# Gate and val of a gated MLP made for two token blocks together, on 512-column matmuls, with w_out2 fetched from DRAM

## The chip, the cores and the metric

One core of one Trainium2 chip runs the whole program. The metric is the device time of one execution in microseconds (us). PE is TensorE (the matrix engine), DVE is VectorE, ACT is ScalarE, POOL is GpSimd; SP is SyncE, whose queue issues all DMA transfers here.

## The reference, cut to what matters

A linear attention makes the 4608 x 512 matrix x; two MLPs follow. Their weights come as 64-bit floats.

```python
# first MLP: w_in 512 x 2048, w_out 2048 x 512
h = x @ w_in
x = (h * np.clip(h + 3.0, 0.0, 6.0) / 6.0) @ w_out
# second MLP: w_gate, w_val 512 x 1536, w_out2 1536 x 512
xn = x / np.sqrt(np.mean(x * x, axis=-1, keepdims=True) + 1e-06) * rms_g
g = xn @ w_gate
val = xn @ w_val
return (g * (1.0 / (1.0 + np.exp(-g))) * val) @ w_out
```

## The kernel before, in words

**Precision.** Each matmul operand is split in a high part (rounded to the matmul's format by ACT, `hi_of`, L197) and a low part (what is left, subtracted by DVE or POOL, `lo_of`, L203). A product of two operands is three matmuls: high with high, high with low, low with high (`PAIRS`).

**Blocks and stages.** The tokens stand in nine blocks of 512 columns. The first 936 us hold the attention, the conversion of the weights from 64 bits, the first MLP (`m1`, `prod1`, `m2`) and the norm of each block (`y_...`, L672 to L706), which is stored to DRAM as `xn_d`. From about 936 us on runs the stage that the change is about: gate, val, silu(gate) x val, and the product with `w_out2` (`m4`), block after block.

**Seven products in place of eight.** Gate and val are made by a Winograd scheme. A pair `i` (of six) takes two chunks of 128 output columns of both w_gate and w_val. Over the halves of the 512 inputs, the two chunks and the two halves of the tokens it is a 2 x 2 by 2 x 2 product, done with seven products `prod(j, i, k)`, k in the order 1, 6, 5, 2, 7, 3, 4. Block `j` of 512 tokens has token halves of 256 columns, and one product makes gate and val side by side in one PSUM bank: 2 (gate, val) x 2 (128-row input chunks) x 3 = 12 matmuls of 256 columns. The weight operand of product k (a sum of parts of w_gate and w_val) is fetched from DRAM as `pg` and split into `phu` and `plu`; seven of the 42 stay in SBUF for all blocks, the others are fetched and split again for each block. The operand from the tokens is one of `xb` and `ut` (sums of parts of xn), split into `xhu` and `xlu`.

**What hangs on a product.** The sums go into three PSUM banks, `pux` (products 1 and 2), `puy` (6, 7, 4) and `puz` (5, 3). After product 1 ACT copies pux (`c_copy`, L838); DVE adds puy to that copy as c12 (after 6), puz as c22 (after 5), puy to c22 (after 7), puz to c12 (after 3), and puy to c21 (after 4), all `c_add` (L845). Product 7 waits for the first c12, product 3 for the first c22, **product 4 for the second c22**, since each of them writes on into the bank that was read. Then come silu on ACT (L868), the multiplication (L873) and the split of the result u into `uh` and `ul`.

**w_out2.** Its 12 chunks of 128 rows lie in SBUF as `hout` and `lout` for the whole stage. `m4(j, i)` multiplies chunk i: 4 token groups x 3 = 12 matmuls of 512 columns, into four PSUM banks `o`.

**What sets the order.** PE's steps are written out in the list `seq`; a chunk step stands after products 2 and 4 of each pair (`merge`). Everything else is a task with needs, a duration and a due step; `Plan.emit` places the tasks on the engines by these numbers as the program is built, and each engine and the SP queue then run their instructions in that order. Rooms are counted there too: 77 SBUF tiles of 2 KB a partition (`unit`), 8 of 4 KB (`wide`), four rotating PSUM banks. `step(h - n)` lets a task begin n steps of `seq` ahead of step h. LEAD, XLEAD and WLEAD are such leads.

Of the kernel before, what the change touches and what calls it, by code (L numbers as in the profile page):

```python
# [24 lines left out]
XLEAD = 2  # L25
WLEAD = 10
# [102 lines left out]
def kernel(  # L129
# [21 lines left out]
    B, H, S, D = q.shape  # L151
# [7 lines left out]
    T = S // P  # L159
    TAIL = S - T * P  # L160
    NP1 = NF // 4
    NP2 = NF2 // 2
    HALF = NB // 2
    EPS = 1e-9
# [288 lines left out]
    def runs(j):  # L453

        done = 0
        while done < P:
            b, s = divmod(j * NB + done * NQ, S)
            step = min(P - done, (S - s) // NQ)
            yield done, done + step, b, s
            done += step  # L460
# [244 lines left out]
    def y_store(j, c):  # L705
# [28 lines left out]
        "u": [(i, k) for k in (4, 3, 7, 2, 5, 6, 1) for i in range(NP2)][:7],  # L734
# [23 lines left out]
    def couples(i):  # L758

        gone = [[k for k in c if (i, k) not in KEEP["u"]] for c in ((1, 6), (5, 2), (7, 3), (4,))]  # L760
        return [(k,) for k in ORDER if (i, k) in KEEP["u"]] + [tuple(c) for c in gone if c]
# [12 lines left out]
    def p_src(l, j, i, k):  # L774
        return wsrc(l, i, k) if l == "h" else pw[j, i, k]

    def p_hi(l, j, i, k):
# [5 lines left out]
        hi_of(wp[l, j, i, k][0], p_src(l, j, i, k))  # L783

    def p_lo(l, j, i, k, eng):
# [3 lines left out]
        lo_of(w[1], p_src(l, j, i, k), w[0], eng)  # L789
# [40 lines left out]
    def prod(j, i, k):  # L830
        product("u", j, i, k)

    def bank(l, j, i, n):
        return pb[l, j, i, n].rearrange("p z t -> p (z t)")

    def c_copy(l, j, i):
        cs[l, j, i, "c21"] = utile(f"c21{l}{j}_{i}")
        nc.scalar.copy(cs[l, j, i, "c21"], bank(l, j, i, "x"))  # L838

    def c_add(l, j, i, n, src, b):  # L840

# [11 lines left out]
    def load_xn(j, k, t):  # L853
# [10 lines left out]
    def u_silu(j, i, m, t):  # L864
# [465 lines left out]
```

## Time and profile before

| | |
|---|---|
| median of three runs | 1779.71 us (1774.97 to 1780.66) |
| profiled execution, its own time | 1777.19 us |
| its span, first to last instruction | 1775.4 us |
| mean granted TensorE clock | 0.994 |
| PE, weight loads, DVE, ACT, POOL busy | 97%, 87%, 77%, 53%, 15% of the span |

The profile is one execution of the program, with every instruction's start and duration. Of an engine's row the name is read as output<-inputs, with buffer numbers left out; "idle before" is the time in which the engine had nothing to do just before the row, with what released it. Durations of matmuls overlap, so what one costs is the distance from its start to the next one's. A granted clock of 1.00 is TensorE's level of 2.4 GHz, 0.50 that of 1.2 GHz; between them a stretch holds both.

### The profile page before, as it was taken

Reading aid. Unit: us, or ns where it says so; the run is one execution under the profiler, and the core shown is the slowest. Engines: PE = TensorE matmul, PEld = TensorE weight load, DVE = VectorE, ACT = ScalarE, POOL = GpSimd, SP = SyncE. Lnnn points to the kernel's source line nnn. Section 1 sums busy time; section 2 is a strip of 40 time slices with the busy share of each in tenths; the row PEclk is TensorE's granted clock in tenths of the full one; section 3 lists DMA queues with packets and bytes.
Section 4 is the critical chain, followed back from the end, with each engine's and each line's share of the span. In section 5 each row is a group of like instructions: output and inputs, shape, how many; then the busy total and the mean of one; then the engine's idle time right before and its main releaser. Section 6 shows DMA issues by size and latency. Waiting matters only on the chain.

```text
span 1775.4 us, 30493 instructions
## 1 busy us (share of the span) xinstructions
PE 1724.4 (97%) x11166; PEld 1543.7 (87%) x11166; DVE 1375.3 (77%) x2670; ACT 944.0 (53%) x2190; POOL 263.5 (15%) x254
## 2 busy tenths in 40 slices
PE   4899999999999999999999999999999999999999
PEld 3678878888888898888889899999999999999998
DVE  8897888888888888788686776767686768676764
ACT  7864566475565656555566444545444545454442
POOL 3254321011313223131111000000000000000000
PEclk9899999999999999999999999999999999999999
DMA  9656486996989888786872442424151524334230
GB/s 253 187 172 215 142 273 235 335 301 218 283 253 285 261 266 260 226 282 222 313 270 92 171 155 101 144 78 162 62 187 48 176 75 134 122 110 146 96 131 25
DMA packets 166278, 331.26 MB, mean 187 GB/s; under 512 B 23536, under 2 KB 78832, under 8 KB 166128
## 3 DMA queue, kind: packets, MB, share of 16 engines
q1 hardware_dynamic: 166128, 329.31, 56.5%
q8 instruction: 88, 1.44, 0.3%
q14 instruction: 62, 0.51, 0.1%
HBM read 267.91 MB, written 61.34 MB: 185 GB/s over the span
## 4 chain that ended last, share of the span: by engine, by line
PE 82%; DMA 7%; DVE 6%; ACT 2%; SPq 1%; issue 1%; ACTq 0%; DVEq 0%
PE y L655 17%; PE o L891 16%; PE puy L821 13%; PE puz L821 9%; PE pux L821 9%; PE h L596 6%; PE phy L821 4%; PE phz L821 3%; PE phx L821 3%; DMA q<-in_q_dram 2%; PE kvp L404 1%; DMA v<-in_v_dram 1%; DMA k<-in_k_dram 1%; DMA raw_gv<-in_moe_w_val_dram 1%; PE xps L552 1%
## 5 line engine op out<-in xcount | busy, mean ns | idle before, releaser
L203 DVE TENSOR_TENSOR plu<-pg,phu 128x512 fp32r<-128x512 f32 x317 | 217.0, 692 | 59.8 <-ACT phu L197 56.2
L821 PE MATMUL puy<-xhu,phu 128*128 128x256 f32 x648 | 183.5, 283 | 2.6 <-DVE c22u L845 2.6
L197 ACT ACTIVATE phu<-pg 128x512 fp32r<-128x512 f32 x322 | 184.4, 623 | 1.5 <-DMA pg<-pd 1.4
L821 PE MATMUL puy<-xhu,plu 128*128 128x256 f32 x648 | 183.8, 284 | 0.0
L821 PE MATMUL puy<-xlu,phu 128*128 128x256 f32 x648 | 183.8, 284 | 0.0
L891 PE MATMUL o<-hout,uh 128*128 128x512 f32 x432 | 170.2, 394 | 0.0
L891 PE MATMUL o<-lout,uh 128*128 128x512 f32 x432 | 169.6, 393 | 0.0
L891 PE MATMUL o<-hout,ul 128*128 128x512 f32 x432 | 168.4, 390 | 0.1
L655 PE MATMUL y<-gl,hout 128*128 128x512 f32 x360 | 142.3, 395 | 5.4 <-DVE gl L203 5.4
L655 PE MATMUL y<-gh,hout 128*128 128x512 f32 x360 | 144.4, 401 | 0.8 <-ACT ysb L668 0.8
L655 PE MATMUL y<-gh,wo 128*128 128x512 f32 x432 | 142.8, 391 | 0.0
L655 PE MATMUL y<-gh,lout 128*128 128x512 f32 x360 | 141.2, 392 | 0.0
L821 PEld LDWEIGHTS puy<-xhu,phu 128*128 128x128 f32 x648 | 124.4, 192 | 5.0 <-DVE c22u L845 2.8
L821 PEld LDWEIGHTS puy<-xlu,phu 128*128 128x128 f32 x648 | 124.6, 192 | 2.1
L845 DVE TENSOR_TENSOR c22u<-c22u,puy 128x512 f32<-128x512 f32 x54 | 37.1, 687 | 113.3 <-PE puy L821 113.3
L821 PEld LDWEIGHTS puy<-xhu,plu 128*128 128x128 f32 x648 | 124.6, 192 | 0.0
L868 ACT ACTIVATE u<-c22u 128x256 f32<-128x256 f32 x54 | 22.6, 418 | 188.2 <-DVE c22u L845 188.2
L821 PE MATMUL pux<-xhu,plu 128*128 128x256 f32 x432 | 122.3, 283 | 0.0
L821 PE MATMUL puz<-xlu,phu 128*128 128x256 f32 x432 | 122.3, 283 | 0.0
L821 PE MATMUL puz<-xhu,phu 128*128 128x256 f32 x432 | 122.3, 283 | 0.0
L821 PE MATMUL puz<-xhu,plu 128*128 128x256 f32 x432 | 122.2, 283 | 0.0
L821 PE MATMUL pux<-xlu,phu 128*128 128x256 f32 x432 | 122.2, 283 | 0.0
(254 smaller groups left out, 5037.1 us busy)
## 6 DMA issues: line engine op xcount, KB each, us to landing
pg<-pd SPq DMA_DIRECT2D x153, 512.0 KB, 6.1
wh<-rdh SPq DMA_DIRECT2D x126, 512.0 KB, 4.9
wo<-rdout SPq DMA_DIRECT2D x54, 512.0 KB, 4.3
raw_out<-in_moe_w_out_dram SPq DMA_DIRECT2D x28, 512.0 KB, 5.2
rdh<-hw SPq DMA_DIRECT2D x21, 512.0 KB, 4.5
v<-in_v_dram SPq DMA_DIRECT2D x72, 128.0 KB, 5.1
xn_d<-ysb SPq DMA_DIRECT2D x36, 256.0 KB, 3.6
xb<-xn_d SPq DMA_DIRECT2D x36, 256.0 KB, 3.6
```

The source lines that it names most:

```text
L197: nc.scalar.activation(hi, src, AF.Copy)
L203: on(engine).tensor_tensor(lo, src, hi.bitcast(F32), ALU.subtract)
L404: nc.tensor.matmul(ps[e * D:(e + 1) * D, u, s:s + D + 1], kk, vv, start=(u == 0 and t == 0), stop=(t == T), skip_group_check=True,)
L552: nc.tensor.matmul(ps[:, :, p0:p1], kvbd[b % 2][a][:, u, :], t[z][:, :, p0:p1], start=(n == 0), stop=(n == 2),)
L596: nc.tensor.matmul(hps[j, i], w[a][:, o:o + P], xs[j][b][u], start=(u == 0 and m == 0), stop=(u == C - 1 and m == 2),)
L655: nc.tensor.matmul(acc[j][c], w[a][:, c * P:(c + 1) * P], g[b], start=(i == 0 and n == 0), stop=(i == NF - 1 and n == 2),)
L821: nc.tensor.matmul(ps[:, z, :], w[a][:, o:o + P], x[b][:, c * HALF:(c + 1) * HALF], start=(first and z == 0 and c == 0 and m == 0), stop=( ...
L845: nc.vector.tensor_tensor(cs[l, j, i, n], t, bank(l, j, i, b), ALU.add)
L868: nc.scalar.activation(ut[j, ch][:, t * HALF:(t + 1) * HALF], c_part("u", j, i, m, t, 0), AF.Silu)
L891: nc.tensor.matmul(acc["o", j][c], u[a][:, c * P:(c + 1) * P], w[b], start=(i == 0 and n == 0), stop=(i == NF2 - 1 and n == 2),)
```

## The change

Blocks 1 to 8 are taken in four couples (`SUPER`: block 0 alone, then 1 and 2, 3 and 4, 5 and 6, 7 and 8). For a couple, the scheme's two token halves are the two whole blocks, so that a half has 512 columns, and gate (z = 0) and val (z = 1) are products of their own: `prod(S, i, z, k)` is 2 x 3 = 6 matmuls, with 512 columns in a couple and 256 in block 0. Seven products of gate come ahead of seven of val; I call such seven a group. Block 0 has 12 groups, each couple 12.

Weight operands are fetched in DRAM's new layout by half (gate or val) and by two products at once, and split once for each couple; none stays in SBUF. Token operands of a couple are 1024 columns wide and lie in wide tiles. The silu of gate is made while val is computed. The 12 chunks of w_out2 are split into wide tiles during block 0, put to DRAM after their use there, and fetched from there (512 KB each) for each of the eight other blocks. A pair of chunk steps follows from a queue, one pair to a group, and none where none is ready: in block 0 after every second group, in the first couple at first too; the last seven pairs come after all products. Planned durations of PE's steps are raised: `m1`, `m2` and `m4` from 2.6 to 2.73, `prod1` from 1.31 to 1.44.

```diff
-XLEAD = 2
-WLEAD = 10
+XLEAD = 9
+ULEAD = 7
+WLEAD = 9
...
+    SUPER = [(0,), *((j, j + 1) for j in range(1, NJ, 2))]
+    COUPLES = ((1, 6), (5, 2), (7, 3), (4,))
...
-    def p_put(i, ks, z):
+
+
+    def p_put(i, ks, n):
         if (i, ks) not in w_d:
-            w_d[i, ks] = dram.tile([P, len(ks), NB], F32, name=f"pd{i}_{ks[0]}")
-        nc.sync.dma_start(w_d[i, ks][:, z], wsrc("u", i, ks[z]))
-
-    def p_get(j, i, ks):
-        t = wtile(f"pg{j}_{i}_{ks[0]}", F32, (P, len(ks), NB))
-        nc.sync.dma_start(t, w_d[i, ks])
-        for z, k in enumerate(ks):
-            pw[j, i, k] = t[:, z]
-
-    def p_src(l, j, i, k):
-        return wsrc(l, i, k) if l == "h" else pw[j, i, k]
+            w_d[i, ks] = dram.tile([P, 2, len(ks), HALF], F32, name=f"pd{i}_{ks[0]}")
+        nc.sync.dma_start(w_d[i, ks][:, :, n], wsrc("u", i, ks[n]).rearrange("p (z f) -> p z f", z=2))
+
+    def p_get(S, i, z, ks):
+        pw[S, i, z, ks] = utile(f"pg{S}_{i}{z}_{ks[0]}", F32, (P, len(ks), HALF))
+        nc.sync.dma_start(pw[S, i, z, ks], w_d[i, ks][:, z])
+
...
-    def prod(j, i, k):
-        product("u", j, i, k)
+    def prod(S, i, z, k):
+
+        first = k in (1, 6, 5)
+        n = NB if len(SUPER[S]) == 2 else HALF
+        if first:
+            pb["u", S, (i, z), BANK[k]] = ptile(f"pu{BANK[k]}{S}_{i}{z}", (P, n))
+        ps, w, x = pb["u", S, (i, z), BANK[k]], wp["u", S, i, z, k], xo["u", S, k]
+        for c in range(2):
+            for m, (a, b) in enumerate(PAIRS):
+                nc.tensor.matmul(
+                    ps, w[a][:, c * P:(c + 1) * P], x[b][c],
+                    start=(first and c == 0 and m == 0), stop=(c == 1 and m == 2), skip_group_check=True,
+                )
...
+    def load_xn(S, k, t):
+
         n = f"b{k + 1}{t + 1}"
-        xb["u", j, n] = utile(f"x{n}_{j}")
-        nc.sync.dma_start(
-            xb["u", j, n].rearrange("p (c t) -> p c t", c=2),
-            xn_d[j][2 * k:2 * k + 2, :, t * HALF:(t + 1) * HALF].rearrange("c p t -> p c t"),
-        )
+        if len(SUPER[S]) == 2:
+            x = wtile(f"x{n}_{S}", F32, (P, 2, NB))
+            src = xn_d[SUPER[S][t]][2 * k:2 * k + 2]
+        else:
+            x = utile(f"x{n}_{S}", F32, (P, 2, HALF))
+            src = xn_d[SUPER[S][0]][2 * k:2 * k + 2, :, t * HALF:(t + 1) * HALF]
+        nc.sync.dma_start(x, src.rearrange("c p t -> p c t"))
+        xb["u", S, n] = x
...
+    def u_sum(S, n, x, y, eng):
+
+        to = {"t3": "b12", "t4": "t2"}.get(n)
+        if to:
+            xb["u", S, n] = xb["u", S, to]
+        elif len(SUPER[S]) == 2:
+            xb["u", S, n] = wtile(f"u{n}_{S}", F32, (P, 2, NB))
+        else:
+            xb["u", S, n] = utile(f"u{n}_{S}", F32, (P, 2, HALF))
+        on(eng).tensor_tensor(*(xb["u", S, m].rearrange("p c t -> p (c t)") for m in (n, x, y)), ALU.subtract)
...
+    def u_xhi(S, k, c):
+        xo.setdefault(("u", S, k), [[], []])
+        t = utile(f"xhu{S}_{k}{c}", F32R)
+        hi_of(t, u_parts(S, k)[c])
+        uh[S, k, c] = t
+        xo["u", S, k][0] += [t] if len(SUPER[S]) == 2 else [t[:, :HALF], t[:, HALF:]]
...
+    def v_hi(ch):
+        v2 = wt["out2", ch] = wtile(f"wv{ch}", F32R)
...
+    def v_put(ch):
+        r_put(("out2", ch), wt.pop(("out2", ch)), 2)
+
+    def v_get(S, t, ch):
+        wo["v", S, t, ch] = r_get(("out2", ch), f"wv{S}{t}_{ch}")
+
+    def m4(S, t, i):
+        j = SUPER[S][t]
         if i == 0:
             acc["o", j] = [
-        w, u = wt["out2", i], us.pop((j, i))
+        w, u = wo.pop(("v", S, t, i)) if S else [wt["out2", i][:, z] for z in range(2)], us.pop((S, t, i))
...
-    for j in range(NJ):
+
+
+    wait = [(S, t, i) for S, js in enumerate(SUPER) for t in range(len(js)) for i in range(NP2)]
+    group, done = 0, {}
+    for S in range(len(SUPER)):
         for i in range(NP2):
-            late = [(m4, j, i - 1), (m4, j, i - 1 + NP2)] if i else (
-                [(m4, j - 1, NP2 - 1), (m4, j - 1, NF2 - 1)] if j else tail2[NJ - 1])
-            seq += merge([(prod, j, i, n) for n in ORDER], late)
-    seq += [(m4, NJ - 1, NP2 - 1), (m4, NJ - 1, NF2 - 1)]
+            for z in range(2):
+                late = []
+                if S == i == 0:
+                    late = tail2[NJ - 1][2 * z:2 * z + 2]
+                elif done.get((wait[0][0], wait[0][2]), group) < group:
+                    n = wait.pop(0)
+                    late = [(m4, *n), (m4, *n[:2], n[2] + NP2)]
+                seq += merge([(prod, S, i, z, n) for n in ORDER], late)
+                if z:
+                    done[S, i] = group
+                group += 1
+    for n in wait:
+        seq += [(m4, *n), (m4, *n[:2], n[2] + NP2)]
...
-        if kind != "gv":
+            split((n,), [(n, "get"), *step(h - 8)], h - 4, v_hi, v_lo, (i,), first={"w": 1}, take=(), give=U, other=FLEX)
+            plan.add((n, "away"), Q, 2 * DMA_US, v_put, i, needs=[(n, "lo"), (m4, 0, 0, i)], due=h, give={"w": 1}, lag=DMA_LAG)
+            for S in range(1, len(SUPER)):
+                for t in range(2):
+                    hj = pos[m4, S, t, i]
+                    plan.add((n, "get", S, t), Q, 2 * DMA_US, v_get, S, t, i, needs=[(n, "away"), *step(hj - 8)],
+                             due=hj - 4, take={"w": 1}, lag=DMA_LAG)
+        elif kind != "gv":
             split((n,), [(n, "s" if late is None else "get")], h - 4, w_hi, w_lo, n, give=() if kind == "in" else U, other=FLEX)
...
+            give["u"] = 2 * (i == NP1 - 1) + 2 * (j == NJ - 1 and keep)
+        took = 2.73
+        if f is prod1:
+            took = 1.44
+        elif f is prod:
+            took = 1.37 if len(SUPER[a[0]]) == 2 else 0.72
+        plan.add(st, E, took, f, *a, needs=needs, due=h, take=take, give=give, lag=0.2)
```

The planner's order moves on every engine. Three places of it follow; the digits that end a name are the tile's serial number.

PE, in the stage, between products 1 and 6 of a pair, before (the names are weights `phu`, `plu` and tokens `xhu`, `xlu`; each product is four times the first three rows):

```order
L821 MATMUL pux_2_13444<-xhu_1_13051,phu_2_1_13295 128x256
L821 MATMUL pux_2_13444<-xlu_1_13058,phu_2_1_13295 128x256
L821 MATMUL pux_2_13444<-xhu_1_13051,plu_2_1_13300 128x256
L821 MATMUL puy_2_13461<-xhu_6_13054,phu_2_6_13316 128x256
L821 MATMUL puy_2_13461<-xlu_6_13062,phu_2_6_13316 128x256
L821 MATMUL puy_2_13461<-xhu_6_13054,plu_2_6_13323 128x256
```

The same place in the first couple after the change (all six matmuls of product 1 of gate, and half of product 6):

```order
L848 MATMUL pux_10_12409<-xhu_10_12029,phu_10_1_12310 128x512
L848 MATMUL pux_10_12409<-xlu_10_12038,phu_10_1_12310 128x512
L848 MATMUL pux_10_12409<-xhu_10_12029,plu_10_1_12314 128x512
L848 MATMUL pux_10_12409<-xhu_11_12056,phu_10_1_12310 128x512
L848 MATMUL pux_10_12409<-xlu_11_12067,phu_10_1_12310 128x512
L848 MATMUL pux_10_12409<-xhu_11_12056,plu_10_1_12314 128x512
L848 MATMUL puy_10_12418<-xhu_60_12042,phu_10_1_12310 128x512
L848 MATMUL puy_10_12418<-xlu_60_12086,phu_10_1_12310 128x512
L848 MATMUL puy_10_12418<-xhu_60_12042,plu_10_1_12314 128x512
```

A product has six rows in place of twelve, each of 512 columns, and a weight tile serves gate or val alone.

DVE, where the norm of block 8 falls into block 0's products, before, from a row of the norm (`ysb`) to the second c22 of that pair (`wv` below is a split of w_out2, `ul` of u, `plu` of weights):

```order
L703 SCALAR_TENSOR_TENSOR ysb_1_11096<-ysb_1_11096,g_sb,r_11445 128x512
L845 TENSOR_TENSOR c12u_3_11512<-c21u_3_11490,puy_3_11475 128x512
L845 TENSOR_TENSOR c22u_3_11529<-c21u_3_11490,puz_3_11495 128x512
L703 SCALAR_TENSOR_TENSOR ysb_2_11104<-ysb_2_11104,g_sb,r_11445 128x512
L703 SCALAR_TENSOR_TENSOR ysb_3_11102<-ysb_3_11102,g_sb,r_11445 128x512
L203 TENSOR_TENSOR ul_8_11550<-u_8_11409,uh_8_11458 128x512
L203 TENSOR_TENSOR plu_4_1_11553<-pg_4_1_11312,phu_4_1_11473 128x512
L203 TENSOR_TENSOR plu_4_5_11555<-pg_4_5_11351,phu_4_5_11508 128x512
L873 TENSOR_TENSOR u_3_11547<-u_3_11547,pux_3_11460 128x256
L203 TENSOR_TENSOR plu_4_6_11574<-pg_4_1_11312,phu_4_6_11557 128x512
L203 TENSOR_TENSOR plu_4_2_11578<-pg_4_5_11351,phu_4_2_11572 128x512
L845 TENSOR_TENSOR c22u_3_11529<-c22u_3_11529,puy_3_11475 128x512
```

After the change, from the last row of the norm's Newton steps (`r`) to the second c22 of a gate group:

```order
L703 TENSOR_TENSOR r_11265<-r_11265,ra_11294 128x512
L207 TENSOR_TENSOR ul_1_11326<-u_0_1_11112,uh_1_11287 128x512
L870 TENSOR_TENSOR c12u_20_11328<-c21u_20_11292,puy_20_11280 128x256
L707 SCALAR_TENSOR_TENSOR ysb_0_11051<-ysb_0_11051,g_sb,r_11265 128x512
L207 TENSOR_TENSOR wv_11306<-wg_out_10379,wv_11306 128x512
L870 TENSOR_TENSOR c22u_20_11345<-c21u_20_11292,puz_20_11299 128x256
L707 SCALAR_TENSOR_TENSOR ysb_1_11049<-ysb_1_11049,g_sb,r_11265 128x512
L707 SCALAR_TENSOR_TENSOR ysb_2_11064<-ysb_2_11064,g_sb,r_11265 128x512
L207 TENSOR_TENSOR ul_7_11358<-u_0_7_11181,uh_7_11308 128x512
L207 TENSOR_TENSOR plu_21_1_11367<-pg_21_1_11238,phu_21_1_11318 128x512
L707 SCALAR_TENSOR_TENSOR ysb_3_11060<-ysb_3_11060,g_sb,r_11265 128x512
L870 TENSOR_TENSOR c22u_20_11345<-c22u_20_11345,puy_20_11280 128x256
```

The eleven rows between the Newton steps and that c22 are much the same kind of work, with additions of 256 columns and a split of w_out2; but PE has four products of six matmuls and one chunk step ahead of them in place of four of twelve.

DVE, at the end of block 0, from the first c12 to the second c22 of the last pair, before:

```order
L845 TENSOR_TENSOR c12u_5_11883<-c21u_5_11858,puy_5_11843 128x512
L203 TENSOR_TENSOR plu_0_5_11885<-pg_0_5_11717,phu_0_5_11881 128x512
L845 TENSOR_TENSOR c22u_5_11901<-c21u_5_11858,puz_5_11866 128x512
L203 TENSOR_TENSOR plu_0_2_11907<-pg_0_5_11717,phu_0_2_11903 128x512
L873 TENSOR_TENSOR u_5_11921<-u_5_11921,pux_5_11824 128x256
L801 TENSOR_TENSOR ut_1_11924<-xb_1_11899,ut_1_11860 128x512
L801 TENSOR_TENSOR xb_1_11811<-xb_1_11899,xb_1_11811 128x512
L801 TENSOR_TENSOR ut_1_11941<-xb_1_11856,ut_1_11924 128x512
L203 TENSOR_TENSOR plu_0_7_11943<-pg_0_7_11768,phu_0_7_11939 128x512
L845 TENSOR_TENSOR c22u_5_11901<-c22u_5_11901,puy_5_11843 128x512
```

After the change, in the last val group of block 0, up to the second c22:

```order
L899 TENSOR_TENSOR ut_1_12031<-xb_1_11983,ut_1_12011 128x1024
L207 TENSOR_TENSOR xlu_10_12038<-xb_1_11977,xhu_10_12029 128x512
L899 TENSOR_TENSOR xb_1_11952<-xb_1_11983,xb_1_11952 128x1024
L207 TENSOR_TENSOR xlu_11_12067<-xb_1_11977,xhu_11_12056 128x512
L870 TENSOR_TENSOR c12u_51_12080<-c21u_51_12065,puy_51_12058 128x256
L207 TENSOR_TENSOR xlu_60_12086<-ut_1_12031,xhu_60_12042 128x512
L207 TENSOR_TENSOR plu_51_4_12098<-pg_51_4_12035,phu_51_4_12082 128x256
L870 TENSOR_TENSOR c22u_51_12106<-c21u_51_12065,puz_51_12071 128x256
L207 TENSOR_TENSOR plu_00_1_12112<-pg_00_1_12040,phu_00_1_12096 128x512
L207 TENSOR_TENSOR xlu_61_12124<-ut_1_12031,xhu_61_12108 128x512
L207 TENSOR_TENSOR xlu_50_12128<-ut_1_12011,xhu_50_12051 128x512
L870 TENSOR_TENSOR c22u_51_12106<-c22u_51_12106,puy_51_12058 128x256
```

The sums of the next tokens (`ut`, `xb`) are 1024 columns wide, and their splits (`xlu`) stand between this group's additions; before, they stood behind them.

## Rows read from the trace of the kernel before

**Rows 1.** The page: span, and busy time of each engine.

```profile
span 1775.4 us, 30493 instructions
PE 1724.4 (97%) x11166; PEld 1543.7 (87%) x11166; DVE 1375.3 (77%) x2670; ACT 944.0 (53%) x2190; POOL 263.5 (15%) x254
```

**Rows 2.** Stretches: length, busy PE, PEld, DVE, ACT, POOL (instructions), clock, DMA share, GB/s.

```profile
830.00:936.00 106.00, 105.30 (x653) 94.35 (x653) 83.52 (x160) 56.93 (x110) 15.05 (x11) 1.00 0.81 278
936.00:1030.00 94.00, 91.29 (x621) 84.64 (x621) 70.72 (x116) 49.42 (x94) 9.09 (x8) 0.98 0.34 115
1030.00:1123.00 93.00, 93.00 (x648) 87.10 (x647) 65.30 (x113) 43.14 (x86) 2.48 (x2) 1.00 0.36 122
```

**Rows 3.** Waits of PE from 936 us to the end: total, times, longest.

```profile
PE puy L821 <- DVE c22u L845: 2.6, 1, 2.6
```

**Rows 4.** The chain that ended last: start, us, what, number of instructions.

```profile
103.46 70.77 PE h L596 x312
...
937.29 1.44 PE puy L821 x12
...
941.62 2.75 PE o L891 x12
...
1763.51 8.20 PE o L891 x36
```

**Rows 5.** DVE in order of time: start, us, instruction; distances are read from starts.

```profile
955.25 0.68 DVE L203 TENSOR_TENSOR plu<-pg,phu 128x512 fp32r<-128x512 f32 x1
955.85 0.68 DVE L845 TENSOR_TENSOR c22u<-c21u,puz 128x512 f32<-128x512 f32 x1
...
962.60 0.42 DVE L873 TENSOR_TENSOR u<-u,c22u 128x256 f32<-128x256 f32 x1
962.93 0.68 DVE L845 TENSOR_TENSOR c12u<-c12u,puz 128x512 f32<-128x512 f32 x1
```

**Rows 6.** The chain again, at the norm of block 8.

```profile
965.43 1.28 ACT L689
966.72 0.69 ACT r L689
967.43 1.28 ACT L690
968.72 0.64 ACT r L690
...
969.39 0.70 DVE ra L696
...
972.09 0.70 DVE r L699
...
981.62 0.61 DVE c22u L845
...
982.27 2.54 PE puy L821 x12
984.82 3.44 PE o L891 x12
```

**Rows 7.** Two stretches after that wait, columns as in rows 2.

```profile
982.00:984.00 2.00, 1.73 (x10) 1.73 (x11) 1.84 (x4) 1.24 (x3) 0.43 (x1) 0.69 1.05 366
984.00:986.00 2.00, 2.00 (x8) 1.71 (x8) 0.69 (x1) 0.42 (x2) 0.50 (x1) 0.50 0.99 388
```

**Rows 8.** Waits of DVE from 936 us to the end, the longest.

```profile
DVE c22u L845 <- PE puy L821: 110.8, 52, 3.3
```

**Rows 9.** DMA issues on the page: number, size, median us to landing.

```profile
pg<-pd SPq DMA_DIRECT2D x153, 512.0 KB, 6.1
wo<-rdout SPq DMA_DIRECT2D x54, 512.0 KB, 4.3
```

**Rows 10.** Waits of PE from 100 to 936 us, the longest of seven (13.6 us in all).

```profile
PE y L655 <- DVE gl L203: 5.4, 3, 3.5
PE kmb L371 <- DVE kd L365: 3.2, 3, 1.9
```

More of the change, by code (lines that the diff above doesn't have):

```diff
@@ L158 @@
     NJ = NT // NB
-    T = S // P
-    TAIL = S - T * P
+    T = SEQ // P
+    TAIL = SEQ - T * P
     NP1 = NF // 4
@@ L456, in runs @@
         while done < P:
-            b, s = divmod(j * NB + done * NQ, S)
-            step = min(P - done, (S - s) // NQ)
+            b, s = divmod(j * NB + done * NQ, SEQ)
+            step = min(P - done, (SEQ - s) // NQ)
             yield done, done + step, b, s
@@ L1231 @@
         elif f is m4:
-            needs += [(("out2", i), "lo"), (("u", j, i), "lo")]
+            S, t, i = a
+            blocks = [x for js in SUPER for x in js]
+            b = blocks.index(SUPER[S][t])
+            needs += [(("out2", i), "get", S, t) if S else (("out2", i), "lo"), (("u", S, t, i), "lo")]
             if i == 0:
-                needs += [(("o", j - 1), "ev", c) for c in range(C)] if j else [(("y", NJ - 1), "ev", c) for c in range(C)]
+                needs += [(("o", blocks[b - 1]), "ev", c) for c in range(C)] if b else [(("y", NJ - 1), "ev", c) for c in range(C)]
@@ L1235 @@
             give["u"] = 2
-        else:
-            l, groups, home, last = ("h", NP1, SHARE, NJ - 1) if f is prod1 else ("u", NP2, 0, None)
-            p = a[2]
-            keep = (i, p) in KEEP[l]
-            if l == "u":
-                needs.append((("w", 0 if keep else j, i), p, "lo"))
-            elif keep:
-                needs.append((("p", l, i), p, "lo"))
-            else:
-                needs.append((("p", l, i), p, "get", j))
-                give["w"] = 1
-            needs.append((("t", l, j), p, "lo"))
+            give["w"] = int(S > 0)
+        elif f is prod:
+            S, i, z, p = a
+            ks = next(c for c in COUPLES if p in c)
+            needs += [(("w", S, i, z), ks, "lo"), (("t", "u", S), p, "lo")]
@@ L1248 @@
             if p in (1, 6, 5):
                 take["ps"] = 1
-            needs += [(("c", l, j, i), m) for m in {2: ["p1"], 7: ["u2"], 3: ["v"], 4: ["c22"]}.get(p, ())]
-            give["u"] = 2 * (i == groups - 1) + 2 * (not keep and l == "u" or j == last and keep)
-        plan.add(st, E, 1.31 if f in (prod, prod1) else 2.6, f, *a, needs=needs, due=h, take=take, give=give, lag=0.2)
+            needs += [(("c", "u", S, (i, z)), m) for m in {2: ["p1"], 7: ["u2"], 3: ["v"], 4: ["c22"]}.get(p, ())]
@@ new lines @@
+            give["u"] = 2 * (p == ks[-1]) + 2 * len(SUPER[S]) * (i == NP2 - 1 and z)
+        else:
+            p = a[2]
+            keep = (i, p) in KEEP["h"]
+            if keep:
+                needs.append((("p", "h", i), p, "lo"))
+            else:
+                needs.append((("p", "h", i), p, "get", j))
+                give["w"] = 1
+            needs.append((("t", "h", j), p, "lo"))
+            if p in (1, 6, 5):
+                take["ps"] = 1
+            needs += [(("c", "h", j, i), m) for m in {2: ["p1"], 7: ["u2"], 3: ["v"], 4: ["c22"]}.get(p, ())]
+            give["u"] = 2 * (i == NP1 - 1) + 2 * (j == NJ - 1 and keep)
@@ L1275 @@
         p_tasks(i)
-        for j in range(NJ):
-            c_tasks("u", j, i, prod)
+        for S in range(len(SUPER)):
+            for z in range(2):
+                u_tasks(S, i, z)
     for j in range(NJ):
@@ L1284 @@
         norm_tasks(j)
-        xn_tasks(j)
-        o_tasks(j)
+    for S, js in enumerate(SUPER):
+        xn_tasks(S)
+        for t in range(len(js)):
+            o_tasks(S, t)
     with tc.manual_schedule():
```

220 lines of the change are left out of this document (142 added, 78 removed).

## The prediction

> **What bounds the kernel now.** I read the first page first: TensorE (PE) is busy 97% of the span, VectorE (DVE) 77% [rows 1]. A share over the whole span hides stages, so the table by stage comes next [rows 2]. The reader is to see there that in the gate/val/w_out2 stage, which begins near 936 us, PE is busy in every microsecond of a block's 93 us, at full granted clock, while DVE has 65 of 93 and the DMA share is 0.36. The list of PE's waits says the same: from 936 us to the end it names one wait, 2.6 us [rows 3]. So this stage, 840 us or 47% of the span, is bound by how fast PE takes matmuls, and only fewer or cheaper matmuls shorten it. What one costs is read from start to start in the chain that ended last, since a matmul's own duration overlaps the next: twelve matmuls of 256 columns take 1.44 us (0.1198 each), twelve of 512 take 2.75 us between 256-column ones (0.229), 0.2278 each in a run of 36, 0.2268 in a run of 312 [rows 4]. Two narrow ones (0.2396) therefore cost 10 to 13 ns more than the wide one that moves the same columns.
>
> **The change part by part.**
>
> *Products, wide.* Before, 9 blocks x 6 pairs x 7 products x 12 = 4536 matmuls of 256 columns. After, block 0 alone keeps 504 (84 products of 6), and the four couples of blocks have 4 x 84 = 336 products of 6 matmuls with 512 columns: 2016 in place of 4032. Each such product takes 6 x 0.2268 to 0.229 = 1.361 to 1.375 us in place of 1.4375: 336 x 0.0625 to 0.0765 = 21.0 to 25.7 us. The stage will now hold almost nothing but 512-column matmuls, so I take the 0.2278 of the run of 36, 1.367 us: **-23.7 us**.
>
> *The 108 chunk steps with w_out2* (12 matmuls each) are unchanged in number. Their 2.75 us begins with slower first matmuls after narrow ones; in long runs twelve cost 2.72. So 0 to 3 us; I take **-1**.
>
> *Block 0 alone* has the same columns, but its steps are half as long (0.72 us a product), and the work of the other engines falls in the same 93 us. DVE starts its 512-column operations 0.60 us apart and 256-column ones 0.33 apart [rows 5]; the 1024-column subtraction for two blocks stands in no row, and the line through these two puts it at 1.14 (bounds: 0.69, one operation, to 1.37, two full durations). Through most of block 0 the products still hide it: the second c22 addition, which product 4 waits for, has product 3 (0.72 us) as its cover and needs 0.33 plus a hand-over. Two places don't fit.
>
> (1) *The norm of block 8.* Before, this is the only wait [rows 3]: two table loads and two activations on ScalarE (ACT), the Newton steps on DVE from 969.39 to 972.79, and then some 9 us of other rows until c22 ends at 982.23 [rows 6]. After it the clock stood at 0.69 and 0.50 for 4 us [rows 7], so that the next product took 2.54 in place of 1.44 and the next chunk step 3.44 in place of 2.75: 1.8 us more. In the new order the same chain falls into a group (seven products of gate or of val) whose products take 0.72. Worked out from the group's start: the sum of squares now stands on PE ahead of product 4 of the group before and is done 0.7 us before the start, ACT at 2.2, DVE's Newton steps at 5.7, and then eight rows of 0.6 and three of 0.33 follow up to the second c22: 11.5. PE would be there after five 0.72 products, product 3 and a chunk step, at 7.05: a stall of 4.5 us in place of 2.6, the clock's 1.8 paid in both. **+1.9** (bounds: -4.4, no stall and no low clock; +4.5, twice the stall).
>
> (2) *The step from block 0 to the first couple.* Here DVE gets the couple's four 1024-column subtractions and fourteen 512-column splits instead of half of that, beside groups of 5.03 us. The last val group of block 0, which has no chunk step in it, has 17 DVE rows, 2 x 1.14 + 8 x 0.6 + 7 x 0.33 = 9.4 us. DVE begins it some 1.7 us early, during the chunk step ahead of it. By its rows c12 and the first c22 are in time, the second c22 ends 5.55 us into the group where PE wants it at 4.3 (1.25); then product 2 of the couple, which reads xl of operand 2, reaches it 1.8 us too early, and product 4 0.35. **+3.4** (bounds: 0, and 5.6 if DVE begins on time only).
>
> *The three later steps from couple to couple* have the same DVE work beside groups of 9.6 to 15.1 us: 7 to 13.7 us each by their rows, and product 3's cover is 1.37 us. 0, as before, where DVE waited 110.8 us in this stage for PE before the second c22 [rows 8]. If that cover is gone, they cost like (2).
>
> *w_out2's chunks.* 96 fetches of 512 KB on the SP queue are added, 12 puts of the same size too; the weights of the products come in 240 fetches of 256 or 128 KB in place of 153 of 512 and some smaller, because a couple reads them once. A couple moves 10.5 MB of weights, 12.6 of w_out2, 2 of x and 2 of output, 27 MB in some 181 us (84 x 1.367 + 24 x 2.74), 150 GB/s, where the stage ahead of this one moved 278 [rows 2]. A fetch of this size lands in 4.3 to 6.1 us [rows 9] and is issued eight steps ahead (six products and two chunk steps, 13.7 us). 0; a wait would stand on PE.
>
> *The first 936 us.* No operation changes there but the making of w_out2's halves (12 splits, moved into block 0 and counted above) and the puts of the weight sums, whose rows are written in two halves. But the planner's durations for PE steps change (1.31 to 1.44 and 2.6 to 2.73), so the order on every engine is shuffled from about 90 us on. PE's waits there are 13.6 us in all, the longest 3.5 [rows 10]. 0, with 5 us either way.
>
> Sum on the profiled execution's own 1777.2 us: -23.7 - 1 + 1.9 + 3.4 = -19.4, so 1757.8. That execution lies 2.5 us under the median of the runs shown; I split that and say **1759 us**.
>
> **A rule against the trace.** The chain gives a wide matmul 227 to 229 ns and two narrow ones 239.6 [rows 4]. The Trainium skill (TensorE: Matmul & The Clock Gate, Back-to-back issue gap) states N/2.4 + 2.5 ns, from which I estimate 109 for 256 columns and 216 for 512. By it the 2016 matmuls saved are worth 2.5 ns each, 5 us in place of 23.7. The trace disagrees in both widths by 11 to 13 ns for each matmul, and the trace decides.
>
> **The rivals.**
>
> *B: DVE is the bound through block 0 and at every step.* If operations cost their durations (0.69 and 0.42 [rows 5]) and not their distances, groups 1 to 11 of block 0 hold 89 us of DVE work beside 88 us of PE; (1) and (2) double (+5.3), and the six groups without a chunk step lose the 0.69 of the split that stands ahead of c22: 1759 + 5.3 + 4.2 = 1769. For it: DVE has hardly a gap there. Against it: the distances are measured.
>
> *C: the stalls aren't there,* because ACT and DVE run ahead of what I worked out: -4.4 at (1) and 0 at (2) give 1759 - 1.9 - 4.4 - 3.4 = 1749.
>
> *D: these matmuls are paid by the column alone.* Then 512 columns cost as much as twice 256 and nothing is saved: 1759 + 23.7 = 1783, no change. For it: nothing but that no 512-column matmul with these operands has run. Against it: L596 has just such operands (weights stationary, split activations moving) and runs at 0.2268. By the formula of the Trainium skill (TensorE: Matmul & The Clock Gate, Back-to-back issue gap) the time would end near here too, at 1759 + 18.7 = 1778.
>
> *E, slower: w_out2's fetches wait for a place.* There are 8 wide buffers; while a couple's operands are loaded and split, six of them are held, for some 20 of its 108 steps. Two are left for chunks, each held for a landing and a step: (2.75 + 6.1)/2 = 4.4 us a chunk, where PE asks for one each 7.55. It decides from a landing of 14.5 us on: then 18 chunk steps lose 1.06 us each, which is the gain. At 17 us they lose 2.3 each, 42 us: 1759 + 42 = 1801. For it: where DMA share is high, 512 KB take 6 us and the queue is in order, so everything behind waits too. Against it: half that load here.
>
> **How the numbers follow.** My forecast 0.60 (1753 to 1766 by itself: 2 to 3 us from the products' bounds, 5 from the first 936 us), B 0.13, C 0.12, D 0.05, E 0.05; 0.05 for an order of the first 936 us that loses 10 to 20 us. A measurement of this kernel tells about 0.3% (5.3 us) from no change. Faster by more than that: forecast, B and C, 0.85 less 0.02 = 0.83; the same: D and part of the last, 0.09; slower 0.08. The range that leaves out two in ten or fewer goes from C's lower edge to a little above B: 1745 to 1776.
>
> **What would show it.** Right: in the profile after, six product matmuls of 512 columns take 1.36 to 1.375 us from start to start, 2016 of them; a couple's 84 products and 24 chunk steps take some 181 us without a wait of PE; PE's waits name c22 (or ul) near the norm of block 8 and c22 or xl at the end of block 0, 8 us together; DVE's busy share falls. Wrong: distances near 0.24 (D), PE waits for wv from DMA (E), c22 waits in every couple (B), a clock under 1.0 that lasts, or new waits ahead of the stage.

## The result and the profile after

The changed kernel takes 1790.51 us (median of six runs, 1789.33 to 1799.55) where the kernel before took 1777.28 beside it (1772.02 to 1780.66): 1.0084 times as long, 95% interval 1.0058 to 1.011. Forecast were 1759 us and a faster kernel; 1790.5 also lies above the range of 1745 to 1776. Medians here and below are over all executions of a version; of the ten of one (2.6 with 1.44, the third experiment) two took 2118 and 2821 us, and they hardly move its median. The page of its profile, first its span and its busy times [rows 1]:

```profile
span 1788.6 us, 26411 instructions
PE 1711.6 (96%) x9150; PEld 1445.5 (81%) x9150; DVE 1303.7 (73%) x2501; ACT 870.0 (49%) x2018; POOL 260.1 (15%) x259
```

PE has 2016 matmuls fewer and DVE 72 us less to do, as planned, and yet the end is later. Where the time went is told by one landmark, the first product of gate or val in block 0. The lists of the matmuls into pux (duration least, median, greatest; first and last start), before and after:

```profile
L821 PE MATMUL pux<-xhu,phu x432: 277/283/366, 914.7 to 1755.9; 128*128 128x256 f32 x144
```

```profile
L848 PE MATMUL pux<-xhu,phu x240: 277/389/628, 940.8 to 1736.0; 128*128 128x512 f32 x96, 128*128 128x256 f32 x24
```

From that start to the end of the span the stage took 1775.4 - 914.7 = 860.7 us before and 1788.6 - 940.8 = 847.8 after: it gained 12.9. But it began 26.1 us later. The loss lies ahead of the stage, where not one matmul was changed. Stretches of that part (length, busy PE and its matmuls, clock, DMA share, GB/s), before and then after:

```profile
0.00:100.00 100.00, 69.10 (x452) 0.95 0.78 214
100.00:190.00 90.00, 90.00 (x399) 1.00 0.58 190
190.00:330.00 140.00, 135.72 (x653) 0.98 0.70 243
330.00:630.00 300.00, 293.98 (x1987) 1.00 0.85 268
630.00:905.00 275.00, 271.64 (x1742) 1.00 0.82 268
sum 905.00, PE 860.44; mean PE 172.09
```

```profile
0.00:100.00 100.00, 71.68 (x446) 0.91 0.77 209
100.00:190.00 90.00, 86.82 (x373) 0.98 0.58 194
190.00:330.00 140.00, 129.16 (x625) 0.96 0.63 213
330.00:630.00 300.00, 288.90 (x1912) 0.99 0.84 266
630.00:905.00 275.00, 267.88 (x1718) 0.99 0.78 255
sum 905.00, PE 844.45; mean PE 168.89
```

PE is busy 16 us less in 905, in four of the five stretches and most between 190 and 330 us; and in every stretch its granted clock is 0.01 to 0.04 lower. Matmul by matmul up to the landmark (5284 in both kernels), PE's idle times between matmuls sum to 49.6 us in place of 33.4, and the matmuls themselves, from start to start, took 10 us more: the two make the 26. The long stalls cost twice: they are idle time, and the clock falls behind them.

The worst of them shows the manner. PE had finished block 0 of the first MLP at 260 us and needed its banks `y` evacuated by DVE (`ysb`) to go on. PE's row and DVE's rows in order of time in the kernel after:

```profile
270.04 0.77 PE L659 MATMUL y<-gh,hout 128*128 128x512 f32 x1 [8.65 <-DVE ysb L674]
```

```profile
262.88 0.69 DVE L207 TENSOR_TENSOR gl<-gr,gh 128x512 fp32r<-128x512 f32 x1
266.32 0.69 DVE L756 TENSOR_TENSOR swh<-wg_in,wg_in 128x512 f32<-128x512 f32 x1 [2.75 <-DMA wg_in<-wd_in]
266.93 0.69 DVE L207 TENSOR_TENSOR gl<-gr,gh 128x512 fp32r<-128x512 f32 x1
267.53 1.76 DVE L756 TENSOR_TENSOR swh<-swh,wg_in 128x512 f32<-128x512 f32 x1
269.21 1.28 DVE L674 COPY ysb<-y 128x512 f32<-128x512 f32 x2
```

DVE runs its rows in the planned order. Ahead of the evacuation stand a weight sum `swh`, for whose fetched input DVE idles 2.75 us, and two splits `gl` of fetched rows; the sum's second row then takes 1.76 us, beside a row of POOL. The chain that ended last gives the two transfers, and the price after the stall:

```profile
254.06 6.71 DMA gr<-g_d
260.78 5.42 DMA wg_in<-wd_in
...
270.04 5.12 PE y L659 x13
```

The planner counts on 0.73 + 2.3 = 3.03 us for either transfer; in this chain they took 6.7 and 5.4. PE waited 8.65 us, and its next 13 matmuls took 5.12 us in place of 13 x 0.2267 = 2.95, at a granted clock of 0.50 from 270 to 274 us. In the kernel before, where no wait of PE in this part from 100 us on is longer than 3.5 us [rows 10], DVE evacuated `y` ahead of its first weight sum there:

```profile
257.33 1.28 DVE L670 COPY ysb<-y 128x512 f32<-128x512 f32 x2
...
262.07 0.69 DVE L753 TENSOR_TENSOR swh<-wg_in,wg_in 128x512 f32<-128x512 f32 x1
```

The order differs because the change also raised PE's planned durations; that this and nothing else is the cause had to be tested.

### The profile page after: what moved, and what is told of

Same layout as the page of the kernel before. It is cut to its first block, busy times and chain, and to the rows that moved or that the text cites. A ratio compares the mean times of both kernels' runs of the same rounds, so it can differ in the third digit from the quotient of the medians.

```text
span 1788.6 us, 26411 instructions
## 1 busy us (share of the span) xinstructions
PE 1711.6 (96%) x9150; PEld 1445.5 (81%) x9150; DVE 1303.7 (73%) x2501; ACT 870.0 (49%) x2018; POOL 260.1 (15%) x259
## 4 chain that ended last, share of the span: by engine, by line
PE 74%; DVE 12%; DMA 8%; ACT 3%; issue 2%; SPq 1%; POOL 0%; DVEq 0%; ACTq 0%; POOLq 0%
PE y L659 16%; PE o L968 16%; PE puy L848 12%; PE pux L848 8%; PE puz L848 8%; PE phy L830 4%; PE h L600 3%; PE phz L830 3%; PE phx L830 2%; DMA q<-in_q_dram 2%; DMA raw_gv<-in_moe_w_val_dram 2%; PE kvp L408 2%; DMA raw_out<-in_moe_w_out_dram 1%; ACT q L506 1%; DMA v<-in_v_dram 1%
## 5 line engine op out<-in xcount | busy, mean ns | idle before, releaser
L968 PE MATMUL o<-wv,uh 128*128 128x512 f32 x864 | 267.2, 391 | 0.0
L207 DVE TENSOR_TENSOR plu<-pg,phu 128x512 fp32r<-128x512 f32 (+1 forms) x232 | 149.1, 647 | 122.0 <-ACT phu L201 121.8
L968 PEld LDWEIGHTS o<-wv,uh 128*128 128x128 f32 x864 | 162.4, 189 | 33.2
L968 PE MATMUL o<-wv,ul 128*128 128x512 f32 x432 | 168.7, 390 | 1.0 <-DVE ul L207 1.0
L863 ACT COPY c21u<-pux 128x512 f32<-128x512 f32 (+1 forms) x60 | 32.6, 543 | 241.8 <-PE pux L848 241.7
L848 PE MATMUL puy<-xhu,phu 128*128 128x512 f32 (+1 forms) x360 | 134.3, 373 | 7.7 <-DVE c22u L870 7.6
L848 PE MATMUL puy<-xlu,phu 128*128 128x512 f32 (+1 forms) x360 | 132.6, 368 | 0.0
L848 PE MATMUL puy<-xhu,plu 128*128 128x512 f32 (+1 forms) x360 | 132.4, 368 | 0.0
L830 PE MATMUL phy<-xhh,wh 128*128 128x256 f32 x576 | 118.6, 289 | 0.0
L830 PEld LDWEIGHTS phy<-xhh,wh 128*128 128x128 f32 x576 | 95.2, 192 | 3.1 <-issue 1.5
L848 PE MATMUL pux<-xlu,phu 128*128 128x512 f32 (+1 forms) x240 | 89.1, 371 | 2.0 <-DVE xlu L207 2.0
```

Of the source, the lines that this page charges most:

```text
L207: on(engine).tensor_tensor(lo, src, hi.bitcast(F32), ALU.subtract)
L830: nc.tensor.matmul(ps[:, z, :], w[a][:, o:o + P], x[b][:, c * HALF:(c + 1) * HALF], start=(first and z == 0 and c == 0 and m == 0), stop=( ...
L848: nc.tensor.matmul(ps, w[a][:, c * P:(c + 1) * P], x[b][c], start=(first and c == 0 and m == 0), stop=(c == 1 and m == 2), skip_group_chec ...
L968: nc.tensor.matmul(acc["o", j][c], u[a][:, c * P:(c + 1) * P], w[b], start=(i == 0 and n == 0), stop=(i == NF2 - 1 and n == 2),)
```

## The experiments

Theory 1: the raised planned durations (`took`) reshuffle the first part, and that loses the 26 us. Theory 2: the other things moved there do it. Each run is given with its median, and its ratio to the kernel before, run beside it, with the 95% interval.

**One: the old durations back ahead of the stage.**

```diff
-        took = 2.73
+        took = 2.73 if f is m4 else 2.6
         if f is prod1:
-            took = 1.44
+            took = 1.31
```

> The changed kernel with the planner's old durations for the steps ahead of the gate/val stage (2.6 us for a step of the first and second matmul, 1.31 for a product of the first layer; the products of gate and val and the chunk steps keep 1.37 and 2.73). Theory 1, the new durations reshuffle the first part and that loses 26 us there: the first gate/val product starts near 915 us as in the kernel before, and the time is about 1765 us, 0.986 to 0.99 of the kernel before. Theory 2, the loss in the first part comes from what else was moved there (puts in two halves, w_out2's splits, the rooms of unit and wide tiles): the start stays near 940 us and the time near 1790.

1759.85 us, 0.9911 (0.9881 to 0.9941); the stage begins at 910.3 us. Theory 1 holds, theory 2 falls. The same place on DVE in this kernel:

```profile
257.79 1.28 DVE L674 COPY ysb<-y 128x512 f32<-128x512 f32 x2
...
261.98 0.68 DVE L756 TENSOR_TENSOR swh<-wg_in,wg_in 128x512 f32<-128x512 f32 x1
```

The evacuation stands ahead of the sum, which comes 4 us after it, and PE waits 0.2 us for it.

**Two: the new durations in the kernel before,** the other way round: `1.31` to `1.44` and `2.6` to `2.73` in its `plan.add`.

> The kernel before with nothing changed but the planner's durations of PE steps: 1.44 for every product in place of 1.31, 2.73 for every other step in place of 2.6. Theory 1: its first gate/val product starts near 940 us in place of 915 and the time is some 20 to 26 us above the kernel before, 1797 to 1804. Theory 2: no change in the first part, 1775 to 1782.

1804.41 us, 1.0162 (1.0127 to 1.0197); its first gate/val product starts at 944.5 us. A kernel with no other edit loses 29 us, 7.5 of them in one wait for `ysb`. The edit also raises the steps of the stage itself, but that takes 859.8 us, as before (860.7).

**Three and four: one duration back at a time** (2.6 with 1.44, and 2.73 with 1.31).

> The changed kernel with the old 2.6 us for the steps of the first and second matmul, and the new 1.44 for the products of the first layer. Theory 1 in the form that the loss hangs on the 2.6 (all that stands ahead of 330 us and the second matmuls among the products): near 1765 us. In the form that it hangs on the 1.44: near 1790. An order that happens to lose in either: both in between. Theory 2: 1790.

1773.61 us, 0.9984 (0.9964 to 1.0004), stage from 922.4 us.

> The changed kernel with the old 1.31 us for the products of the first layer, and the new 2.73 for the steps of the first and second matmul. Theory 1 in the form that the loss hangs on the 1.31 against 1.44: near 1765 us. In the form that it hangs on the 2.6 against 2.73: near 1790. Theory 2: 1790.

1782.56 us, 1.0041 (1.0021 to 1.0062), stage from 936.0 us; the wait for `ysb` is 8.7 us here, and 1.2 in the third. Either number does harm by itself. In these orders the 2.73 weighs more (22.7 us over the first experiment, against 13.8 for the 1.44).

**Five: the wide matmul alone.** In the first experiment's version a product's matmuls are issued as two of 256 columns; the plan stays the same.

```diff
+        for t in range(n // HALF):
+            s = slice(t * HALF, (t + 1) * HALF)
-                    ps, w[a][:, c * P:(c + 1) * P], x[b][c],
+                        ps[:, s], w[a][:, c * P:(c + 1) * P], x[b][c][:, s],
```

> The version of the first experiment (old durations ahead of the stage, 1759.85 us) in which each 512-column product matmul of a couple is issued as two of 256 columns over the same operands and bank; planned durations and so the order of all else stay the same. If the wide matmul itself is the gain: 336 products at 1.4375 in place of 1.361 us, +25.7, so 1781 to 1786 (a few us of stalls at the steps from couple to couple may hide behind the longer products). Rival, the gain comes from the other changes of the stage (fewer weight splits, fewer rows on DVE): within 5 us of 1760.

1787.26 us, 1.0064 (1.0042 to 1.0087): 27.4 us more than with wide matmuls, so the width is the gain. A product costs 1.44 us again and a chunk step 2.75, by the chain of this kernel:

```profile
1107.01 1.44 PE puy L850 x12
1111.33 2.75 PE o L970 x12
```

**Six: longer landing times in the plan,** with the new PE durations: `DMA_LAG`, the planned time to landing, from 2.3 to 4.5.

> The changed kernel, its new PE durations kept, with the planner's landing time of every transfer raised from 2.3 to 4.5 us beyond the issue (landings measured in its profile are 4 to 7 us). If the loss is that rows fed by late transfers stand on DVE and ACT ahead of rows that PE waits for: the 8.7 us wait for the evacuation of y near 265 us is gone and the time falls to 1765 to 1775. Rival, only the ratio of PE's durations to those of the other engines counts: 1785 to 1795.

1782.63 us, 1.0037 (1.0021 to 1.0053), between the two expectations. The stage begins at 927.5 us, 13 earlier, and the wait for `ysb` is 1.9 us; but the stage now takes 858.4 us in place of 847.8.

**Seven: shorter durations still,** 2.47 and 1.24 in the version of the first.

> The version of the first experiment with planned durations shorter still ahead of the stage: 2.47 us for the steps of the first and second matmul (before 2.6), 1.24 for a product of the first layer (before 1.31). If a plan in which PE comes early puts the rows that PE waits for ahead of others: the same or better, 1750 to 1761. Rival, the old numbers are a lucky spot among orders that mostly lose: 1770 to 1790.

1765.7 us, 0.9938 (0.9915 to 0.996), stage from 917.9. Neither side: shorter is not better without end, but nothing like the loss at 2.73.

**Eight: the other engines' planned durations 5% longer,** with the new PE durations.

```diff
+        us *= 1.05 if engine in ("act", "dve", "pool") else 1
         self.tasks[name] = (engine, us, fn
```

> The changed kernel, its new PE durations kept, with every planned duration on ACT, DVE and POOL raised by 5% (the ratio to PE's durations as before; transfers' times unchanged). If the ratio of PE's durations to the other engines' is what counts: 1760 to 1768. If what counts is how PE's durations stand to the landing times of the transfers: 1780 to 1795.

1792.3 us, 1.01 (1.0072 to 1.0128), stage from 941.1. PE's ratio to ACT and DVE is not what counts here. (The edit leaves the durations planned for rows that may go to POOL instead, `other`, as they were.)

**Nine: one row.** The weight sums of the second pair must come behind the evacuation of `y`.

```diff
+            wait_y = [(("y", 0), "ev", c) for c in range(C)] if i == 1 else []
```

> The changed kernel, all its durations kept, with one added need: the weight sums of one pair of the first layer (the row that waited 2.7 us on DVE for the fetch of wg_in at 266 us) may not be placed ahead of the evacuation of y of block 0. Up to that place the order of rows is that of the changed kernel, with the sums left out. If rows fed by late transfers ahead of that evacuation make the loss: the 8.7 us wait falls to 3 to 6 us (other rows ahead of it hang on fetches of gr), and with the clock after it the time falls by 3 to 9 us, to 1782 to 1787. If the long wait has another cause: 8.7 us again, and 1790.

1784.59 us, 1.0047 (1.003 to 1.0063), as expected: 5.9 less than the changed kernel, and the stage begins at 934.2 in place of 940.8. The 8.65 us at that place have become 3.9, for `qn`, and `ysb` costs 0.2. What is left there is not a fetch, as the expectation had it: ahead of `qn` DVE waits 1.96 us for `q` from ACT.

**Ten and eleven: two durations between,** 2.55 with 1.285 and 2.66 with 1.37.

> The version of the first experiment with 2.55 and 1.285 us planned for PE's steps ahead of the stage, between its 2.6 and 1.31 (1759.85 us) and the 2.47 and 1.24 of the seventh experiment (1765.7). If the time goes smoothly with the planned duration: 1760 to 1766, stage starting at 910 to 918 us. If each order is a draw of its own: anywhere from 1758 to 1785.

1756.24 us, 0.9883 (0.986 to 0.9906).

> The version of the first experiment with 2.66 and 1.37 us planned for PE's steps ahead of the stage, half way between its 2.6 and 1.31 (1759.85 us) and the changed kernel's 2.73 and 1.44 (1790.5). If the time goes smoothly with the planned duration: 1770 to 1780. If each order is a draw of its own: anywhere from 1758 to 1795, and then no rule on the size of the duration follows.

1780.29 us, 1.0011 (0.9997 to 1.0025), with a wait of 6.9 us for `ysb`. The versions that differ in the planned durations ahead of the stage alone, in one table:

| planned step, product (us) | stage begins | stage takes | median |
|---|---|---|---|
| 2.47, 1.24 | 917.9 | 846.0 | 1765.7 |
| 2.55, 1.285 | 907.1 | 847.4 | 1756.24 |
| 2.60, 1.31 | 910.3 | 846.0 | 1759.85 |
| 2.66, 1.37 | 932.7 | 848.9 | 1780.29 |
| 2.73, 1.44 (the change) | 940.8 | 847.8 | 1790.51 |

The stage is the same within 3 us; all the difference stands ahead of it. Up to 2.60 the starts lie within 11 us of one another, beyond it 22 and 30 us later than at 2.60. A start is read from one profile, and the fifth version, whose plan is the first's, has it at 914.0 in place of 910.3: some 4 us of these differences are scatter. The tenth version is the fastest kernel of this study, 1.2% ahead of the one before; it is the best of several orders, not one that a rule picked.

**Twelve: token operands earlier,** `XLEAD` 12 for 9 in the version of the first.

> The version of the first experiment with the splits of a couple's token operands allowed 12 steps ahead of its first product in place of 9. By the prediction's account of the step from block 0 to the first couple (late subtractions and splits on DVE): the 5.0 us of waits there (c22 2.3, xl 2.1, xh 0.6) shrink by some 3 us and the 1.2 to 1.3 us at each later couple too, 1753 to 1758. Rival: the rows only push others on DVE back, so c22 waits longer and the time is 1760 or above.

1762.07 us, 0.9914 (0.9892 to 0.9937): no gain. The waits at the steps are the same (xl 2.1 and xh 0.6 us; c22 8.3 in the stage, where it was 7.6).

**Thirteen: only the transfers planned 5% longer,** 0.77 and 2.42 us, with the new PE durations.

> The changed kernel, its new PE durations kept, with the planned durations of transfers raised by 5% (0.77 us on the queue and 2.42 to land, in place of 0.73 and 2.3), those of ACT, DVE and POOL as they were. If PE's planned durations must stand to the transfers' as before: 1760 to 1770. If to the other engines' and the transfers' together, or to none of them: 1780 to 1795.

1772.18 us, 0.9969 (0.995 to 0.9988), stage from 918.6. Five per cent on the transfers undo 18 of the 31 us, where five per cent on three engines undid nothing.

**Fourteen: transfers and engines 5% longer.**

> The changed kernel, its new PE durations kept, with the planned durations of ACT, DVE and POOL and of the transfers raised by 5%, so that the plan is nearly that of the old durations, stretched by 5% (a few constants are not stretched). If the order follows only from the ratios of all these numbers: near the 1760 us of the first experiment, at most 1768. If the stretch itself, or the products of the first layer (raised by 10%), leaves a loss: 1770 to 1790.

1779.29 us, 1.0006 (0.9988 to 1.0024), stage from 922.8. Less than the transfers alone, so no simple law of ratios holds either (the `other` durations were not stretched here, as in the eighth).

**Fifteen: the long landing time ahead of the stage only.**

> The changed kernel with the landing time planned at 4.5 in place of 2.3 us for all transfers but those of the gate/val/w_out2 stage (in the sixth experiment, with 4.5 for all, the stage began at 927.5 in place of 940.8 us but took 858 in place of 848). If both halves of that came from where they stood: stage from 925 to 930 us, 848 long, so 1772 to 1779. If the first part's half was a draw of the order: 1785 or above.

1772.23 us, 0.9988 (0.9969 to 1.0007); the stage begins at 925.6 and takes 847.9. Both halves of the sixth stood where it said.

**Sixteen: durations too short in the stage as well,** on the tenth version.

> The version of the tenth experiment (2.55 and 1.285 us planned ahead of the stage, 1756.24 us) with the stage's own planned durations shortened too, below what they take: 1.30 in place of 1.37 us for a wide product, 0.68 for 0.72, 2.6 for 2.73 for a chunk step. If planning PE's steps a little too short puts the rows that PE waits for ahead of the others there as well: the 12 us of waits in the stage shrink by some 3 to 6, 1750 to 1754. Rival, the waits at the norm and at the steps from couple to couple are DVE's and ACT's own work, whatever the order: 1755 to 1759.

1762.95 us, 0.9917 (0.989 to 0.9944): 6.7 us more than the tenth. The stage's waits are there as before (c22 8.2 us, ul 2.8 where it was 1.0). This shortening doesn't remove them, nor did the longer lead of the twelfth; that no order would is not shown.

## Why the prediction was wrong

**The step that failed** is the term for the first 936 us: "0, with 5 us either way". It measured 26.1 us. The text saw that the planned durations change the order of every engine there, and priced that by the waits of the order before [rows 10]. But those 13.6 us were the waits of that one order; the new order has its own, 32.6 us from 100 us to the landmark, and the clock loss behind them. The chance of 0.05 for "an order of the first 936 us that loses 10 to 20 us" named the right case, and was too low and too short. With the old durations the same change takes 1759.85 us, and there the term would have been -4.4 (914.7 to 910.3).

Why longer planned steps lose is settled in part. Shown is that the loss comes and goes with them in both kernels (first and second experiment); that at the worst place a weight sum that waits for its fetch stands ahead of a row that PE waits for; that moving the sums of that pair back gives 5.9 us; and that longer planned transfers give back 18 (thirteenth, fifteenth). From 100 us to the landmark DVE and ACT together waited 103 to 115 us for DMA in the six versions whose stage begins after 930 us, and 46 to 89 in the others, but for the fourteenth (108). Yet not every stall is of that kind: ahead of PE's waits of 2.67 us at 146 us and 2.79 at 400 DVE waited for no transfer, but was busy with rows of other work that stood ahead in its order. Since 2.73 is what a step takes, the old 2.6 was an error, on the same side as the transfers' error, which are planned at 3 us and land mostly in 4 to 7. That the two had balanced, and that mending one without the other made the plan worse, is my reading, not shown: the fourteenth speaks against any simple ratio, and what the remaining 12 us hang on stays open.

**The wide products, -23.7.** Right in its mechanism, somewhat more in size. The chain of the kernel after:

```profile
1736.81 2.72 PE o L968 x12
...
1742.25 1.36 PE puy L848 x6
1743.61 40.81 PE o L968 x180
```

A product of six takes 1.36 us, the least that was allowed for: 336 x (1.4375 - 1.36) = 26.0 us, 13 ns for each of the 2016 matmuls saved. The fifth experiment gives 27.4 for the width, chunk steps included. Rival D falls with it. The formula of the Trainium skill (TensorE: Matmul & The Clock Gate, Back-to-back issue gap), which the page gives for the gap of an isolated matmul and by which I estimated 5 us for the same, is not borne out in these streams: 226.7 ns for 512 columns in place of its 216, and 120 for 256 in place of 109.

**The chunk steps, -1.** 2.72 in place of 2.75 us in the couples and the tail: 98 x 0.03 = 2.9 us, the far end of the bound.

**The norm of block 8, +1.9.** It came out slightly the other way. PE's waits of the kernel after from 905 us on (all of them):

```profile
PE puy L848 <- DVE c22u L870: 7.6, 6, 2.3
PE pux L848 <- DVE xlu L207: 2.0, 2, 1.9
PE o L968 <- DVE ul L207: 1.0, 1, 1.0
PE pux L848 <- ACT c21u L863: 0.9, 2, 0.6
PE pux L848 <- ACT xhu L201: 0.6, 1, 0.6
```

Between 980 and 990 us three of them stand (c21 0.65, ul 1.02, c22 1.46), 3.1 us together in place of the 4.5 worked out, and the clock did not fall as it had before [rows 7]:

```profile
980.00:985.00 5.00, 3.33 (x22) 1.00 0.00 0
985.00:990.00 5.00, 3.54 (x23) 1.00 0.62 234
990.00:995.00 5.00, 5.00 (x32) 1.00 0.96 323
```

So the clock's 1.8, which the term had paid in both kernels, fell away. A wait costs more than its listed length, though (the 1.46 here is 1.72 us from start to start): from start to start, against 0.1198 and 0.2267 us a matmul, the place (the sum of squares with it) costs 4.5 us where it had cost 4.9: -0.4.

**The step from block 0 to the first couple, +3.4.** Named rightly (c22, then xl), too small: waits of 2.3, 0.6 and 1.9 us, and here the clock fell, which the term had left out. From the chain and the stretches:

```profile
1048.12 0.97 PE puy L848 x6
1049.09 2.57 PE pux L848 x6
...
1059.93 4.05 PE o L968 x12
1063.98 0.23 PE puy L848
```

```profile
1050.00:1055.00 5.00, 5.00 (x17) 0.77 0.09 33
...
1060.00:1065.00 5.00, 5.00 (x18) 0.74 0.17 65
```

From the start of the wait for c22, 2.3 us ahead of 1048.12, to 1063.98 us PE did product 4 of block 0 (0.72), four products of the couple (5.44) and a chunk step (2.72): 8.9 us of work in 18.2. So +9.3. Part of the wait for c22 stands in a row that the term didn't have. DVE, up to that c22, and POOL:

```profile
1045.29 2.36 DVE L207 TENSOR_TENSOR xlu<-ut,xhu 128x512 fp32r<-128x512 f32 x2
1047.57 0.41 DVE L870 TENSOR_TENSOR c22u<-c22u,puy 128x256 f32<-128x256 f32 x1
```

```profile
1045.70 1.40 POOL L207 TENSOR_TENSOR wv<-wg_out,wv 128x512 fp32r<-128x512 f32 x1 [104.81 <-ACT wv L201]
```

Two such splits take 1.28 us elsewhere; beside a row of POOL they took 2.36, 1.08 more. With the 1.25 that was worked out from DVE's rows alone that is the 2.3. The 1.14 us estimated for a 1024-column subtraction was right (1037.99 to 1039.13).

**The later steps, 0.** Three waits for c22 of 1.3, 1.2 and 1.2 us, one at each, and one of 0.2: 4.9 us from start to start. The cover of 1.36 us was thought enough. Here too DVE's rows ahead of c22 are stretched beside POOL: at the first of these steps a split `plu` takes 2.89 us, at the other two a split `xlu` 1.41, in place of 0.69.

```profile
1198.51 2.89 DVE L207 TENSOR_TENSOR plu<-pg,phu 128x512 fp32r<-128x512 f32 x1
```

```profile
1198.09 2.76 POOL L899 TENSOR_TENSOR ut<-xb,ut 128x1024 f32<-128x1024 f32 x1
```

No run took these rows off POOL, so what they cost is read from rows and not tested.

**The fetches of w_out2, 0.** Right: none of the waits above names `wv`; rival E falls. Rival B too: c22 is late at the norm and at the steps, not in every group. Summed from start to start over the whole stage, PE lost 8.3 us against 0.1198 and 0.2267 us a matmul before and 20.9 after: 9.5 at the step to the first couple, 4.9 at the later steps, 4.5 at the norm, 1.3 at four short waits in block 0 and 0.7 elsewhere (the chunk steps' slow starts are in the 8.3). With 0.5 us more behind the last matmul, 26.0 - 12.6 - 0.5 gives the 12.9 that the stage gained (14.7 in the first experiment).

The number 1759 and the 1759.85 of the first experiment agree by luck, through two errors that cancel: the stage gave 4.7 us less than the 19.4 forecast, and the first part 4.4 more.

## What to carry to other kernels

Where a planner orders the rows, a change of its durations is a change of the whole kernel: price it apart from the rest, and make it apart. A truer number in one place can make the plan worse; look at which rows stand ahead of what the bounding engine waits for, those fed by transfers first, since an engine that runs its rows in order hands a transfer's lateness on. Look also for rows that another engine stretches. And take a stall as its length plus what the clock loses behind it.

## What was unexpected of the hardware

One wait of 2.62 us at the norm brought the granted clock down to 0.50 [rows 6, 7], and one of 8.65 us let 13 matmuls take 5.12 us; three waits of 0.65, 1.02 and 1.46 us within 8 us, with matmuls between them, left it at 1.00. In runs of its own width a 512-column matmul of split operands costs 0.2267 us alike in products, chunk steps and the first MLP (1.36/6, 40.81/180, [rows 4]); between 256-column ones it was 0.229. And DVE's 512-column `TENSOR_TENSOR` rows never took more than 0.70 us in the kernel after where no row of POOL ran at the same time (1022 rows), while of the 243 that had one beside them 62 took more than 1.0 us, up to 2.89.
